# One hand-written list of steps replaced by another: attention and a Mish feed-forward on one core

## The chip, the cores and the metric

The kernel runs on one core of one Trainium2 chip. The metric is the device time of one execution in microseconds (us), the median of the runs. Lower is better.

## The reference, cut to what matters

Eight batches of eight heads go through attention in which a query sees few keys: in heads 0 to 3 the 32 latest positions, in heads 4 to 7 every fourth of the 128 latest. The result, 4608 tokens of 512 features, goes through a feed-forward layer with the Mish function.

```python
batch, n_heads, seq, head_dim = (8, 8, 576, 64)
mask_plain = (rel >= 0) & (rel < window)                                   # window = 32
mask_dil = (rel >= 0) & (rel < window * dilation) & (rel % dilation == 0)  # dilation = 4
scores = np.where(masks[None, :, :, :], scores, -1000000000.0)
attn = np.exp(scores - max) / (sum + 1e-09)
x = (attn @ v), tokens x 512
h = x @ w_in                        # 512 -> 2048
g = h * np.tanh(np.log1p(np.exp(np.minimum(h, 20.0))))
out = g @ w_out                     # 2048 -> 512
```

q, k and v come as 4-byte floats, w_in and w_out as 8-byte floats. The output has the precision of 4-byte floats, so large products are made of f16 halves: a high and a low part of each operand, three products for one.

## The kernel before, in words

**Units.** The work is cut into 16 units u, one for each half (288 positions) of each batch. A unit goes through these steps, each a Python function that issues a few instructions. Some are generators, and every further call of one issues its next piece:

- `ld`, `lv`: the loads of q, k and v. `pr` (`prep`, lines 440 to 540): scales, and the f16 halves of q, k, v; on ScalarE lines 508, 511, 517 and 536.
- `sp` (line 596 on TensorE), `sc` (scores to VectorE, maxima at line 626), `ex` (exponentials, ScalarE line 667 or 654), `tp` (transposes), `va` (line 744 or 738), `tx` (the attention result turned for the next product), one of each for a pair of heads. Units 0 to 3 are "direct": they use 4-byte products, since the f16 halves are not there so early.
- `ff` u.fp (`ff1`, line 840): two row blocks of `x @ w_in`, 12 products of 128x288 each, into both halves of one PSUM tile, then Mish on ScalarE (line 843). `gt` (`gate`, lines 859 and 861): the f16 halves of g.
- `fo` u.e.j (`ff2`, line 871): 12 products of `g @ w_out` for the output block e (0 to 3) and the quarter j of the inner dimension (0 to 3). Blocks 0 and 1 share one PSUM tile, blocks 2 and 3 another, each block one half (bank) of it. After j = 3 a second call moves the block to SBUF (`y`, ScalarE line 885, in four cases VectorE line 883), a third one stores it.
- `wl`, `wm`, `ww`, `ws`, `wp`: loads of the weights and their conversion from 8-byte floats to two f16 halves. On VectorE that is lines 380, 382, 383 and 395, on ScalarE lines 337 and 392.
- `kw` n (`keep_warm`, line 900): n products of zeros of 128x128 on TensorE, whose result nobody reads.

**PSUM.** All of these share four PSUM tiles, `banks`, named b0 to b3, each of two banks:

```python
banks = [ps.tile([P, 2, 512], F32, name=f"b{i}", bufs=1) for i in range(4)]
def take(name, tiles):
    turns[name] = place[0] if place else (turns.get(name, -1) + 1) % len(tiles)
    return tiles[turns[name]]
```

**Order.** No scheduler chooses: the list ORDER at the head of the file names the steps in the order in which they are issued, and each engine runs its instructions in that order. An entry such as `sp2.3=0` also says which of the four PSUM tiles the step takes. The waits between engines are put in by the framework from the tiles that an instruction reads and writes. The loop at the end walks the list:

```python
for name in ORDER:
    name, _, at = name.partition("=")
    place[:] = [int(at)] if at else []
```

In `ff2` both blocks of a pair write the same tile:

```python
if (e, j) == (e & 2, 0):
    d["po", e // 2] = take("b", banks)
po = d["po", e // 2][:, e % 2]
```

Of the kernel before, what the change touches and what calls it, by code (L numbers as in the profile page):

```python
# [42 lines left out]
va0.2 kw6=3 tx0.3 ex0.1 va0.2 sp1.1=3 tx0.3 sc1.1 sp1.2=2 sc1.2 tx0.2=0 tx0.2 tp0.1=1 wl0.2.0 wp0.0.1 kw10=3 sp1.0=3
sc1.0 tp0.1 va0.1=1 tx0.2 tx0.2 va0.1 va0.1 wl0.1.1 ex1.1 kw16=2 kw16=2 kw6=2 tp1.1=2 tp1.1 wm0.2.0 kw10=0 tx0.1=0
tx0.1 kw16=1 kw11=1 tx0.1 tx0.1 tx0.0=1 tx0.0 kw13=2 tx0.0 tx0.0 ww0.1.0 ww0.2.0 ww0.2.0 wm0.1.1 ex1.2 kw16=2 kw16=2
kw16=2 kw2=2 tp1.2=2 tp1.2 ww0.1.1 ww0.1.1 ex1.0 sp1.3=0 sc1.3 ex1.3 ws0.2=1 ws0.2 wp0.2.0 ww0.2.1 wp0.2.1 ws0.1=2
ws0.1 wp0.1.0 xa1 ld2 kw3=3 sp2.0=3 sc2.0 ex2.0 lv2 fs0 ff0.6=1 ff0.6 ff0.6 ff0.7=0 ff0.7 ff0.7 wp0.2.1 wl1.3.1
# [20 lines left out]
pr5 lv5 pr5 fo0.0.3 ff2.6=3 ff2.7=1 ff2.7 ff2.7 ff2.6 ff2.6 gt2.3=2 gt2.3 sc4.3 ex4.3 tp4.3=1 tp4.3 tp4.3=1 fs4
fo2.2.0=0 fo2.3.0 fo2.3.1 fo2.3.2 pr5=1 pr5 fo2.0.0=3 fo2.1.0 fs3 fo2.0.1 fo2.0.2 fo2.0.3 fo2.0.3 fo2.0.3 pr5 pr5 pr5
pr5 pr5 sp4.1=2 sc4.1 ex4.1 tp4.1=2 fo2.3.3 fo2.3.3 fo2.3.3 sp4.0=1 sc4.0 ex4.0 tp4.0=1 tp4.0 tp4.0=2 tx3.3=2 tx3.3  # L70
fo2.2.1 fo2.2.2 fo2.2.3 fo2.2.3 fo2.2.3 fo1.0.0=1 fo1.0.1 fo1.0.2 fo1.0.3 pr5 pr5 fo1.1.0 ld6 pr5 pr5 pr6 pr6 pr6
tx3.3 tx3.3 ff3.0=0 ff3.0 ff3.0 ff3.2=2 ff3.2 ff3.2 fo2.1.1 fo2.1.2 fo2.1.3 fo2.1.3 tp4.1 sp5.1=0 sp4.2=2 sc4.2 ex4.2
tp4.2=1 fo1.1.1 fo1.1.2 sc5.1 va4.3=3 sp5.3=2 sc5.3 va4.3 va4.3 ff3.1=0 ff3.1 ff3.1 gt3.0=3 gt3.0 ff3.3=2 ff3.3 ff3.3
gt3.1=1 fo2.1.3 fo1.0.3 fo1.1.3 lv6 pr6 pr6 pr6 tp4.1=0 va4.1=0 fo1.1.3 ex5.1 tp5.1=0 va4.1 va4.1 tx4.1=1 gt3.1 tx4.1
tx4.1 fo1.0.3 tp4.2 tp4.2=1 tx4.3=0 tx4.3 tx4.3 ff3.6=3 ff3.6 ff3.7=2 ff3.7 ff3.7 tp5.1 tp5.1=0 fo1.1.3 ff3.6 gt3.3=4
gt3.3 pr6 pr6 pr6 pr6 pr6 ff3.4=1 ff3.5=0 ff3.5 ff3.5 ff3.4 ff3.4 gt3.2=0 gt3.2 fo3.2.0=2 fo3.2.1 fo3.3.0 ld7 pr7 pr7
ex5.3 tp5.3=2 tp5.3 fo3.3.1 fs6 fo3.0.0=3 va4.0=0 tp5.3=2 va4.0 va4.0 tx4.0=1 tx4.0 tx4.0 fo3.1.0 fo3.1.1 sp6.1=1
# [5 lines left out]
tx5.0 va5.2=0 va5.2 tx5.3 tx5.3 ex6.2 tp6.2=2 tp6.2 tp6.2=2 va5.2 fo3.0.3 ff4.4=3 ff4.5=1 ff4.5 ff4.5 ff4.4 ff4.4
gt4.2=0 gt4.2 fo4.0.0=2 fo4.0.1 fo4.1.0 fo4.1.1 fo4.1.2 fo4.0.2 pr7 pr7 pr7 pr7 sp7.1=0 sc7.1 sp7.2=1 sc7.2 pr7
sp7.3=3 sc7.3 ex7.1 tp7.1=1 fo4.1.3 fo4.1.3 tx5.2=0 tx5.2 tx5.2 fo4.2.0=0 fo4.2.1 fo4.2.2 fo4.2.3 fo4.2.3 fo4.2.3
fo4.3.0 fo4.1.3 sp6.3=1 ex6.1 tp6.1=0 tp6.1 tp6.1=1 sc6.3 ex6.3 tp6.3=2 tp6.3 tp6.3=0 fo4.3.1 fo4.3.2 fo4.3.3 fo4.3.3
fo4.3.3 sp6.0=3 sc6.0 ex7.3 va6.2=1 va6.2 va6.2 tx6.2=1 ex6.0 ld8 fo4.0.3 fo4.0.3 tx6.2 tx6.2 fo4.0.3 pr8 tp6.0=0 pr8
# [871 lines left out]
```

## Time and profile before

| | |
|---|---|
| median of 3 runs | 964.04 us (962.53 to 965.33) |
| the profiled execution | 965.67 us, span of its instructions 963.7 us |
| mean granted TensorE clock | 0.987 |
| TensorE busy | 919.5 us, 95% of the span |
| VectorE busy | 592.6 us, 61% |
| ScalarE busy | 548.4 us, 57% |
| DMA queue of the program | 80.97 MB, 34.1% of 16 engines' span |

In the rows of the profile, PE is TensorE's matmul side, PEld its loading of weights, DVE is VectorE, ACT ScalarE, POOL GpSimd. A row of the timeline gives start, length, engine, line, operation, what is written and read, and in brackets how long the engine sat idle before it and what ended that. A row of the waits gives the engine and line that waited, what it waited for, the total, the number of times and the longest. In the table by stretches, PEclk is the clock that TensorE was granted, as a share of full speed. The chain of waits gives start, length and what took that time.

### The profile page before, as it was taken

To read this page: it belongs to the slowest core of one execution; us is meant where nothing else is said; L and a number is where in the kernel's file an instruction comes from. 1 tells how busy PE (TensorE), PEld (TensorE's weight loads), DVE (VectorE), ACT (ScalarE), POOL (GpSimd) and SP (SyncE) were. 2 spreads that over 40 slices of the span, in tenths; PEclk is the share of its full clock that TensorE was granted. 3 is DMA by queue.
4 is the path that set the end of the run, shared out by engine and by line. 5 is a ranking of instruction groups with operands and counts; after the bars stand their busy time and mean duration, and the time that the engine had idled before them with its cause. 6 is when DMAs were issued, how large, how long until landed. Compare 5 with 4: busy or idle time off the path is not lost.

```text
span 963.7 us, 21536 instructions
## 1 busy us (share of the span) xinstructions
PE 919.5 (95%) x9278; PEld 736.8 (76%) x9278; DVE 592.6 (61%) x879; ACT 548.4 (57%) x808; POOL 20.6 (2%) x99
## 2 busy tenths in 40 slices
PE   6899999998999999999998999999989999989998
PEld 4788888876878878788777878787867678768776
DVE  3896888575577675777785865665656366234120
ACT  3677675575383756676674655756364554744241
POOL 1000000210000000000000000000000000000000
PEclk9999999998999999999999999999989999999999
DMA  7756135032342324345344333172334121131200
GB/s 252 222 148 198 53 132 131 14 101 52 91 108 64 64 53 108 63 129 109 79 97 92 88 83 58 35 159 47 85 87 94 30 50 38 34 71 14 58 1 25
DMA packets 156558, 82.33 MB, mean 85 GB/s; under 512 B 122960, under 2 KB 152368, under 8 KB 156464
## 3 DMA queue, kind: packets, MB, share of 16 engines
q1 hardware_dynamic: 156464, 80.97, 34.1%
q8 instruction: 72, 1.18, 0.5%
q14 instruction: 22, 0.18, 0.1%
HBM read 49.02 MB, written 9.44 MB: 61 GB/s over the span
## 4 chain that ended last, share of the span: by engine, by line
PE 88%; ACT 5%; DVE 3%; issue 2%; DMA 1%; SPq 0%; POOL 0%; ACTq 0%; DVEq 0%; POOLq 0%
PE b L871 37%; PE b L840 37%; PE b L596 4%; PE b L744 3%; PE b L738 2%; PE b L900 2%; ACT y L885 1%; PE b L715 1%; PE b L593 1%; ACT g L859 1%; DMA knd<-in_kdT 1%; DVE nm L626 0%; ACT sb L667 0%; DVE sb L620 0%; PE b L348 0%
## 5 line engine op out<-in xcount | busy, mean ns | idle before, releaser
L871 PE MATMUL b<-g,w 128*128 128x288 f16 x3072 | 398.5, 290 | 27.7 <-ACT y L885 17.7
L840 PE MATMUL b<-x,w 128*128 128x288 f16 x3072 | 385.4, 286 | 0.0
L871 PEld LDWEIGHTS <-w 128*128 128x128 f16 x3072 | 300.6, 99 | 109.6 <-issue 30.0
L840 PEld LDWEIGHTS <-w 128*128 128x128 f16 x3072 | 298.4, 98 | 75.7
L861 DVE SCALAR_TENSOR_TENSOR g<-hm,sg,g 128x1152 f16<-128x1152 f32 x64 | 90.2, 1415 | 133.0 <-ACT g L859 132.8
L843 ACT ACTIVATE hm<-b,fs 128x576 f32<-128x576 f32 x128 | 92.6, 737 | 119.2 <-PE b L840 114.8
L885 ACT ACTIVATE y<-b,fo 128x288 f32<-128x288 f32 x60 | 42.1, 715 | 87.7 <-PE b L871 83.3
L859 ACT ACTIVATE g<-hm,sg 128x1152 f16<-128x1152 f32 x64 | 80.2, 1254 | 3.0 <-PE b L871 1.3
L667 ACT ACTIVATE sb<-sb,ln_p 72x576 f32<-72x576 f32 (+3 forms) x48 | 42.5, 890 | 42.6 <-DVE sb L628 42.4
L628 DVE TENSOR_TENSOR sb<-sb,nm 72x576 f32<-72x576 f32 (+4 forms) x60 | 45.3, 754 | 2.1
L626 DVE TENSOR_REDUCE nm<-sb 72x8 f32<-72x576 f32 (+4 forms) x60 | 44.9, 748 | 1.6
L620 DVE SCALAR_TENSOR_TENSOR sb<-b,sc,m_d 72x576 f32<-72x576 f32 (+1 forms) x24 | 22.6, 943 | 35.0 <-PE b L596 34.9
L759 DVE TENSOR_TENSOR xs<-b,rec 96x384 f32<-96x384 f32 (+1 forms) x64 | 39.7, 620 | 6.4 <-DVE rec L758 0.5
L620 DVE SCALAR_TENSOR_TENSOR sb<-b,sc,m_r 96x704 f32<-96x704 f32 (+1 forms) x24 | 23.4, 977 | 30.5 <-PE b L596 30.4
L705 DVE TENSOR_TENSOR p<-sb,p 72x576 f16<-72x576 f32 (+3 forms) x32 | 28.6, 898 | 15.9 <-ACT p L703 15.8
L843 ACT ACT_TABLE_LOAD x24 | 30.8, 1283 | 10.0 <-PE b L840 9.7
L596 PEld LDWEIGHTS <-q 64*72 64x72 f16 (+1 forms) x1008 | 25.9, 116 | 8.1 <-issue 7.8
L596 PE MATMUL b<-k,q 64*96 64x128 f16 (+3 forms) x1008 | 30.9, 210 | 0.0
L775 ACT CAST x<-xs 96x384 f16<-96x384 f32 (+1 forms) x27 | 15.1, 557 | 27.0 <-DVE xs L759 18.6
L754 ACT ACTIVATE den<-b 72x8 f32<-72x8 f32 (+1 forms) x48 | 7.9, 167 | 36.8 <-PE b L744 36.8
L758 DVE RECIPROCAL rec<-den 96x6 f32<-96x6 f32 (+1 forms) x64 | 12.0, 188 | 26.6 <-ACT den L754 22.4
L900 PE MATMUL b<-zeros 128*128 128x128 f16 x338 | 25.2, 235 | 3.2 <-ACT x L801 1.1
(140 smaller groups left out, 849.8 us busy)
## 6 DMA issues: line engine op xcount, KB each, us to landing
qn<-in_qT SPq DMA_DIRECT2D x16, 576.0 KB
out_T<-y SPq DMA_DIRECT2D x64, 144.0 KB
raw<-in_w_in SPq DMA_DIRECT2D x16, 512.0 KB
raw<-in_w_out SPq DMA_DIRECT2D x16, 512.0 KB
vn<-in_v SPq DMA_DIRECT2D x48, 128.0 KB
knd<-in_kdT SPq DMA_DIRECT2D x16, 208.0 KB
vdn<-in_vd SPq DMA_DIRECT2D x32, 104.0 KB
knp<-in_kT SPq DMA_DIRECT2D x8, 320.0 KB
```

The costliest lines, as they stand in the source:

```text
L596: nc.tensor.matmul(o, q, k, start=start, stop=stop, skip_group_check=True)
L620: nc.vector.scalar_tensor_tensor(args[0], args[1], d["sc"][:nq], args[2], ALU.mult, ALU.add)
L626: nc.vector.tensor_reduce(nm[:nq, :, j:j + n], x, axis=AX.X, op=ALU.max, negate=True)
L628: nc.vector.tensor_tensor(blocked(sb, c0, n, w), x, nm[:nq, :, j:j + n].unsqueeze(3).broadcast_to([nq, 2, n, w]), op=ALU.add)
L667: nc.scalar.activation(x, x, AF.Exp, bias=ln_p[:nq])
L840: nc.tensor.matmul(ph[:, h, :HT], w1[j][:, c, wi, k * P:(k + 1) * P], x_of(d, xi, c), start=(n == 0), stop=(n == len(seq) - 1))
L843: nc.scalar.activation(d["m"][j][:, k0:k0 + 2], ph[:, :, :HT], AF.Mish, scale=d["fs"][:, j:j + 1])
L859: nc.scalar.activation(g[:, 0], m, AF.Identity, scale=sg)
L861: nc.vector.scalar_tensor_tensor(g[:, 1], m, sg, g[:, 0], ALU.mult, ALU.subtract)
L871: nc.tensor.matmul(po[:, :HT], w2[:, e, j, wi, k * P:(k + 1) * P], d["g"][j][:, gi, k, :], start=(j == 0 and n == 0), stop=(j == NCH - 1 a ...
L885: nc.scalar.activation(o, src, AF.Identity, scale=fo)
L900: nc.tensor.matmul(warm[:, 1, 512 - P:], zeros, zeros, start=True, stop=True)
```

## The change

The list ORDER is replaced by another one. Nothing else differs: the functions, the tiles, the sizes and the engine of each step are the same. The old list has 2051 entries, the new one 2054. The three more are `kw` entries: 30 of them with 338 products of zeros before, 33 with 345 products now. Ahead of the first `sp` step there were 47 of these products, and there are 35. The new list was found by a search whose model takes a PSUM tile of two banks as one thing for waits.

```diff
 ORDER = """
-wl0.3.0 wm0.3.0 ww0.3.0 ww0.3.0 wl0.3.1 wm0.3.1 ww0.3.1 ld0 ww0.3.1 kw16=0 kw16=0 kw15=0 sp0.2=0 sc0.2 ws0.3=1 sp0.1=2
...
+ld0 kw16=0 kw16=0 kw3=0 sp0.1=0 sp0.2=1 sc0.1 sc0.2 sp0.0=2 sc0.0 sp0.3=3 sc0.3 wl0.3.0 wm0.3.0 ex0.2 ww0.3.0 ww0.3.0
```

How blocks of `fo` that share a tile stand to each other differs all through the list. In the old one the work on one block goes on, 25 times, behind the `y` of the other block of its tile, often with little between; around unit 7, for instance, `fo7.3.3 fo7.3.3 fo7.3.3 va8.1 tx8.1=0 tx8.1 tx8.1 pr11 pr11 pr11 fo7.2.1`. In the new one the even block of each of the 32 tiles is ended, with its `y`, before the odd one begins, with steps of other kinds or other tiles between, as in `fo7.2.3 fo7.2.3 fo7.2.3 sp10.0=2 sc10.0 va8.1=0 pr10 tp9.3=1 va8.1 pr10 lv11 va9.0=3 va9.0 va8.1 tx8.1=1 tx8.1 tx8.1 fo7.3.0`.

The first place is ScalarE while the output of unit 2 is made. Before, the queue stands as follows; `y` is the output block, the number behind `<-b` the PSUM tile, `qn`, `q2` and `k2` belong to the `pr` step of a later unit, `sb` and `p161` to its attention:

```order
L885 ACTIVATE y_2894<-b3_73,fo_1696 128x288
L508 ACTIVATE qn_2680<-qn_2680,s_2688 128x1152
L511 CAST q2_2905<-qn_2680 128x288 x2
L511 CAST q2_2905<-qn_2680 128x576
L517 ACTIVATE k2_2910<-knp_2682,s_2688 128x640
L517 ACTIVATE k2_2910<-knd_2684,s_2688 128x832
L667 ACTIVATE sb_2931<-sb_2931,ln_p_121 96x2x352
L703 CAST p161_2505<-sb_2931 96x2x352
L885 ACTIVATE y_2953<-b0_70,fo_1696 128x288
```

Now, on the same engine in the same unit:

```order
L885 ACTIVATE y_2923<-b3_73,fo_1623 128x288
L885 ACTIVATE y_2956<-b0_70,fo_1623 128x288
L508 ACTIVATE qn_2599<-qn_2599,s_2629 128x1152
L511 CAST q2_3018<-qn_2599 128x288 x2
L511 CAST q2_3018<-qn_2599 128x576
L517 ACTIVATE k2_3023<-knp_2601,s_2629 128x640
L517 ACTIVATE k2_3023<-knd_2603,s_2629 128x832
L536 ACTIVATE vh_3031<-vn_2616,s_2629 128x12x64
L536 ACTIVATE vdh_3032<-vdn_2617,s_2629 104x16x64
L843 ACTIVATE hm_2884<-b2_72,fs_2865 128x576
```

The `y` of tile b0 stood behind the whole `pr` step; it now stands ahead of it.

The second place is the head of VectorE's queue. `nm` are the maxima of unit 0's scores, `w13` and `raw` belong to the first weights. Before:

```order
L293 MEMSET ones_111 128x1
L891 MEMSET ln_p_121 128x1
L895 MEMSET zeros_123 128x64
L380 TENSOR_SCALAR w13_105<-w13_105 128x1024
L382 SCALAR_TENSOR_TENSOR raw_127<-raw_127,w13_105 128x1024
L383 SCALAR_TENSOR_TENSOR raw_127<-raw_127 128x1024
```

Now:

```order
L895 MEMSET zeros_123 128x64
L626 TENSOR_REDUCE nm_187<-b0_70 96x2x2
L626 TENSOR_REDUCE nm_187<-b0_70 96x2
L626 TENSOR_REDUCE nm_190<-b1_71 72x8
L626 TENSOR_REDUCE nm_200<-b2_72 96x2x2
L626 TENSOR_REDUCE nm_200<-b2_72 96x2
L626 TENSOR_REDUCE nm_213<-b3_73 72x8
L380 TENSOR_SCALAR w13_105<-w13_105 128x1024
L382 SCALAR_TENSOR_TENSOR raw_215<-raw_215,w13_105 128x1024
L383 SCALAR_TENSOR_TENSOR raw_215<-raw_215 128x1024
```

The conversion of the first weights moved behind all the maxima of unit 0.

More of the change, by code (lines that the diff above doesn't have):

```diff
@@ L43 @@
[L43 to L47, printed above, removed]
@@ L68 @@
[L68 to L72, printed above, removed]
@@ L73 @@
[L73 to L77, printed above, removed]
@@ L83 @@
[L83 to L87, printed above, removed]
@@ new lines @@
+fo2.3.0 fo2.3.1 fo2.3.2 fo2.3.3 fo2.3.3 ex4.1 fo2.1.3 pr6 pr6 pr6 pr6 pr6 pr6 fo2.3.3 sp4.2=2 sc4.2 xa6 ex4.3 tp4.3=1
+tp4.3 tp4.3=1 sp5.2=1 fo1.0.0=3 fo1.0.1 fo1.0.2 fo1.0.3 fo1.0.3 fo1.0.3 sp4.0=0 sc4.0 ex4.0 tp4.0=2 tp4.0 tp4.0=2
+sc5.2 ff3.1=2 ff3.1 ff3.1 gt3.0=1 gt3.0 fo1.1.0 fo1.1.1 fo1.1.2 fo1.1.3 fo1.1.3 fo1.1.3 pr6 pr6 pr6 pr6 pr6 ld7 pr7
+ff3.4=0 ff3.5=2 ff3.5 ff3.5 ff3.4 ff3.4 gt3.2=3 gt3.2 ff3.6=1 ff3.6 ff3.6 ff3.7=3 ff3.7 ff3.7 gt3.3=2 gt3.3 va4.0=2
+va4.0 va4.0 ff3.3=0 ff3.3 ff3.3 gt3.1=0 gt3.1 fo3.2.0=1 fo3.0.0=3 tx4.0=1 tx4.0 tx4.0 tp4.1=1 tp4.1 tp4.1=0 ex4.2
@@ new lines @@
+gt4.1 sp6.2=1 sc6.2 va5.0=0 va5.0 va5.0 tp5.2=0 ff4.1 ff4.1 gt4.0=1 gt4.0 va5.3=2 va5.3 va5.3 tp6.1=2 ff4.6=1 ff4.6
+ff4.7=3 ff4.6 xa5 tx5.0=1 tx5.0 tx5.3=0 tx5.3 tx5.3 tx5.0 va5.2=0 va5.2 va5.2 va5.1=1 va5.1 va5.1 ff4.7 ff4.7 gt4.3=0
+gt4.3 pr7 tp6.1 tp6.1=2 sp6.0=2 sc6.0 ex6.2 tp6.2=0 tp6.2 tp6.2=0 ff4.4=0 ff4.5=1 ff4.5 ff4.4 ff4.5 ff4.4 gt4.2=3
+gt4.2 fo4.2.0=3 fo4.2.1 fo4.0.0=2 fo4.0.1 fo4.0.2 fo4.0.3 fo4.2.2 pr7 pr7 pr7 pr7 sp7.3=1 pr7 ld8 sc7.3 tx5.2=0 tx5.2
+tx5.2 fo4.2.3 sp6.3=0 sc6.3 tx5.1=1 tx5.1 sp7.1=1 sc7.1 fo4.0.3 pr8 fo4.0.3 fo4.1.0 fo4.2.3 fo4.2.3 fo4.3.0 ex6.3
@@ new lines @@
+tx12.3=1 tx12.3 tx12.3 pr13 pr13 lv14 ff11.5 ff11.5 ff11.4 pr14 gt10.3 ff11.6=1 ff11.6 ff11.6 ff11.7=3 ff11.7 ff11.7
+fo10.2.0=2 fo10.2.1 fo10.2.2 fo10.2.3 tx12.2 ex13.3 tp13.3=2 tp12.0=0 va12.0=0 va12.0 fo10.2.3 fo10.2.3 sp13.1=1
+sc13.1 fo10.0.0=3 fo10.0.1 fo10.0.2 fo10.0.3 va12.0 tp13.3 pr14 pr14 fo10.0.3 fo10.0.3 ex13.0 tp13.0=0 tp13.0 tp13.0=2
+ex13.1 tp13.1=1 fo10.3.0 va12.1=1 va12.1 tx12.0=1 tx12.0 tx12.0 fs13 fo10.1.0 gt11.3=4 fo10.1.1 fo10.1.2 fo10.1.3
+fo10.1.3 gt11.3 fo10.3.1 gt11.1=2 gt11.1 fo10.3.2 fo10.3.3 fo10.3.3 gt11.2=0 gt11.2 fo11.0.0=0 fo11.2.0=3 fo11.0.1
@@ new lines @@
+fo11.0.2 fo11.0.3 ex13.2 tp13.2=0 fo11.2.1 fo11.2.2 fo11.2.3 va12.1 tx12.1=1 tx12.1 pr14 pr14 fo10.3.3 fo11.0.3
+fo11.0.3 tx12.2 xa13 tp13.1 tp13.1=0 fo11.1.0 fo11.1.1 pr14 tx12.1 pr14 pr14 sp14.0=2 pr14 pr14 va13.0=1 fo11.2.3
+fo11.2.3 fo11.3.0 sc14.0 va13.1=2 va13.1 va13.1 tp13.3=1 tx13.1=0 fo10.1.3 va13.0 ex14.0 va13.0 fo11.3.1 fo11.3.2
+fo11.3.3 fo11.3.3 sp14.2=2 sc14.2 ex14.2 fo11.1.2 tp13.2 sp14.1=1 sc14.1 ex14.1 tp14.1=1 ld15 lv15 pr15 pr15 pr15 pr15
+pr15 pr15 tp13.2=2 ff12.0=3 ff12.0 ff12.0 tp14.1 ff12.1=2 ff12.1 ff12.1 tp14.2=2 tp14.2 tp14.2=0 tp14.0=0 tp14.0
@@ new lines @@
+fo11.3.3 gt12.0=1 xa14 ff12.2=1 ff12.2 ff12.2 ff12.3=3 ff12.3 ff12.3 gt12.1=3 gt12.1 tx13.0=1 tx13.0 va13.3=2 va13.3
+va13.3 tx13.0 pr15 pr15 fo11.1.3 fo11.1.3 ff12.4=1 ff12.5=3 ff12.5 ff12.5 ff12.4 ff12.4 gt12.2=2 gt12.0 tx13.1
+va14.2=2 va14.2 va14.2 tx13.1 fo11.1.3 tx13.3=1 tx13.3 tx13.3 va13.2=0 va13.2 va13.2 tx13.2=0 tx13.2 gt12.2 ff12.6=3
+ff12.7=1 ff12.7 ff12.7 ff12.6 ff12.6 gt12.3=0 gt12.3 fo12.0.0=2 fo12.0.1 fo12.0.2 fo12.0.3 fo12.2.0=0 fo12.0.3
+fo12.1.0 fo12.1.1 fo12.1.2 tp14.1=1 pr15 pr15 pr15 pr15 tx14.2=1 tp14.0=0 tx13.2 tx14.2 sp14.3=1 sc14.3 fo12.1.3
@@ new lines @@
+sp15.2=1 sc15.2 ex15.2 tp15.2=0 tp15.2 tp15.2=0 ff13.6=0 ff13.7=3 ff13.7 ff13.7 ff13.6 ff13.6 gt13.3=2 gt13.3 fs14
+ff14.0=2 ff14.0 ff14.0 ff14.2=1 ff14.1=3 ff14.2 ff14.2 ff14.1 tp15.0=2 gt13.1 ff14.6=0 ff14.6 tp15.3=2 va15.3=2 va15.3
+va15.3 ex15.1 tp15.1=0 tp15.1 tp15.1=1 fo13.2.0=1 fo13.2.1 fo13.2.2 ff14.6 ff14.1 ff14.3=2 tp15.0 gt14.0=0 gt14.0
+tp15.0=2 ff14.4=0 ff14.3 ff14.3 tx15.3=1 tx15.3 ff14.4 ff14.4 fo13.2.3 fo13.2.3 fo13.2.3 ff14.5=3 ff14.5 va15.1=2
+va15.1 va15.1 tx15.1=0 tx15.1 tx15.1 tx15.3 fo13.0.0=0 fo13.0.1 fo13.0.2 va15.2=2 va15.2 ff14.5 fo13.0.3 fo13.0.3
@@ L165 @@
+ff15.6 fo13.3.3 fo13.3.3 fo13.3.3 ff15.1=3 ff15.1 ff15.1 gt15.0=4 gt15.0 ff15.3=2 ff15.3 ff15.3 gt15.1=3 gt15.1
+ff15.7=0 ff15.7 ff15.7 gt15.3=1 gt15.3 fo15.2.0=1 fo15.0.0=3 fo15.0.1 fo15.2.1 fo15.2.2 fo15.2.3 fo15.2.3 fo15.0.2
+fo15.0.3 fo15.0.3 fo15.3.0 fo15.3.1 fo15.3.2 fo15.2.3 fo15.3.3 fo15.3.3 fo15.0.3 fo15.3.3 fo15.1.0 fo15.1.1 fo15.1.2
+fo15.1.3 fo15.1.3 fo15.1.3
 """.split()
```

198 lines of the change are left out of this document (92 added, 106 removed).

## The prediction

> **What bounds the kernel now.** I read the page first, then TensorE's waits, then its timeline at single waits, then the chain and the clock.
>
> ```profile
> span 963.7 us, 21536 instructions
> PE 919.5 (95%) x9278; PEld 736.8 (76%) x9278; DVE 592.6 (61%) x879; ACT 548.4 (57%) x808; POOL 20.6 (2%) x99
> ...
> L871 PE MATMUL b<-g,w 128*128 128x288 f16 x3072 | 398.5, 290 | 27.7 <-ACT y L885 17.7
> L840 PE MATMUL b<-x,w 128*128 128x288 f16 x3072 | 385.4, 286 | 0.0
> ```
>
> TensorE (PE) is busy for 919.5 of 963.7 us, so the order of steps can only win what lies outside those 919.5 us, which is 44.2 us, and whatever of the busy time is slow or useless. The two feed-forward products make up 784 us of it. They are alike in shape, yet one never waits and the other waits 27.7 us. So the question is what line 871 waits for. The waits of PE alone, from 100 us to the end:
>
> ```profile
> PE b L871 <- ACT y L885: 17.7, 11, 4.6
> PE b L871 <- ACT den L754: 6.2, 2, 3.9
> PE b L871 <- ACT fs L824: 2.5, 1, 2.5
> PE b L871 <- DVE y L883: 1.3, 1, 1.3
> ```
>
> This is the whole answer for that stretch: after 100 us PE waits 15 times, 27.7 us in all, only at line 871, and 12 of the 15 times by name for `y`, the move of a finished output block out of PSUM. (The other three, `den` and `fs`, are small ScalarE instructions that stand behind a `y` in its queue: in the old list the waiting products are `fo10.0.1`, `fo11.0.1` and `fo13.0.2`, which follow the `y` of block 1 of their tile. I count them as the same wait.) The last wait of the program shows which block it is:
>
> ```profile
> 955.75 1.63 PE L871 MATMUL b<-g,w 128*128 128x288 f16 x12
> ...
> 957.47 0.77 ACT L885 ACTIVATE y<-b,fo 128x288 f32<-128x288 f32 x1 [9.03 <-PE b L871]
> ...
> 958.28 1.63 PE L871 MATMUL b<-g,w 128*128 128x288 f16 x12 [0.90 <-ACT y L885]
> ```
>
> In the old list the last products are `fo15.3.3`, and the `y` just before them is that of `fo15.2.3`. Block 2 and block 3 have different banks, and nothing of block 3 is read by the `y` of block 2. Still PE stands idle until it ends. So the program's waits go by the tile of two banks. That is a wait with no other sense, and it costs 0.90 us where ScalarE is free at once. Where ScalarE has a queue, it costs more. Here is the longest one, from the timeline of both engines:
>
> ```profile
> 224.42 1.25 ACT L508 ACTIVATE qn<-qn,s 128x1152 f32<-128x1152 f32 x1 [0.63 <-DVE s L286]
> ...
> 226.27 0.47 PE L786 MATMUL b<-ident,xs 72*128 72x72 f32 x4
> ...
> 228.25 0.97 ACT L517 ACTIVATE k<-knd,s 128x832 f16<-128x832 f32 x1
> ...
> 230.76 0.49 ACT L885 ACTIVATE y<-b,fo 128x288 f32<-128x288 f32 x1
> ...
> 231.30 4.88 PE L871 MATMUL b<-g,w 128*128 128x288 f16 x21 [4.56 <-ACT y L885]
> ```
>
> The `y` of b0 stands behind `qn`, `q2` and `k2` of a later unit, which is the queue shown in the first place of the change. PE loses 4.56 us. And it loses more after that, since its clock falls:
>
> ```profile
> 220.00:240.00 20.00, 15.44 (x135) 11.39 (x134) 11.79 (x24) 11.41 (x16) 0.00 (x0) 0.83 0.22 50
> 500.00:520.00 20.00, 16.32 (x148) 12.49 (x146) 13.31 (x24) 13.02 (x20) 0.78 (x6) 0.91 0.62 121
> 700.00:720.00 20.00, 16.06 (x130) 11.99 (x128) 13.50 (x16) 14.24 (x20) 0.29 (x4) 0.83 0.21 55
> 740.00:760.00 20.00, 17.77 (x173) 13.76 (x168) 5.00 (x8) 6.94 (x10) 0.00 (x0) 0.91 0.07 23
> 840.00:860.00 20.00, 16.27 (x151) 12.23 (x149) 8.75 (x11) 8.52 (x14) 0.00 (x0) 0.92 0.42 86
> ```
>
> The third number from the end of a row is PEclk. It falls below full speed in these five stretches, each of which holds one of the long waits at line 871. The chain shows what the same work takes there:
>
> ```profile
> 133.00 4.41 PE b L871 x36
> 231.30 14.06 PE b L871 x96
> 508.54 6.24 PE b L871 x36
> 708.50 7.04 PE b L871 x36
> 751.22 6.18 PE b L871 x36
> 858.97 24.26 PE b L840 x192
> 911.81 23.52 PE b L840 x192
> ```
>
> **The change part by part.**
>
> *The waits for `y` (a gain of 27.7 us, less what is left).* In the new list each of the 32 even blocks is ended and its `y` issued before the odd block of that tile begins. So 32 places can wait. What hides each is the PE work between the last product of the even block and the first of the odd one. The least of it is at `fo8.0.3` (a `va` and an `sp` step, 18 to 24 products each) and at units 12 and 14 (one `fo`, 12 products).
>
> ```profile
> 255.91 1.05 PE b L596 x42
> 320.52 1.29 PE b L744 x42
> ```
>
> At 1.05/42 and 1.29/42 us a product, 24 of each make 0.6 + 0.7 = 1.3 us. Twelve feed-forward products are 4.41/3 = 1.47 us. Both are more than the 0.90 us that a free ScalarE takes. In the old list 8 such places have no other PE work between at all. If ScalarE is late by its queue, cover of this size doesn't do: at 231.30 PE had 18 products of line 596 and 4 of line 786 to do, and still waited 4.56 us. But in the new list `pr` and its like stand behind the `y`, as the first place shows. Nine of the 32 places have less than 2.2 us of cover by my count of the list. I allow **1.5 us** for them together, a sixth of a microsecond each. The bounds are 0 (all hidden) and 32 x 0.90 = 29 us (no cover works).
>
> *The clock (a gain of 10.4 us).* At full speed 36 products take 4.41 us, so 96 take 11.76 us. The excess is 14.06 - 11.76 = 2.30, 6.24 - 4.41 = 1.83, 7.04 - 4.41 = 2.63 and 6.18 - 4.41 = 1.77 us, together 8.53. The fifth is the wait before 856.41:
>
> ```profile
> 856.41 2.56 PE L871 MATMUL b<-g,w 128*128 128x288 f16 x12 [2.54 <-ACT fs L824]
> ...
> 624.94 1.63 PE L871 MATMUL b<-g,w 128*128 128x288 f16 x12 [1.81 <-ACT y L885]
> ```
>
> Twelve products took 2.56 us there, against 1.63 in the same form of row elsewhere, which is 0.93 more, and the 192 behind them 24.26 - 23.52 = 0.74 more. The sum is 10.2; I take **10.2 us**. The wait of 1.81 us at 624.94 left the clock whole, the one of 2.54 us did not. If no wait of over 2 us is left in the new order, all 10.2 us come back. If two are, some 4 of them stay lost.
>
> The Trainium skill ("TensorE: Matmul & The Clock Gate", Part 1: The HAM clock gate) says that the clock falls to half after an idle window of about 3.4 us. By that rule alone the wait of 2.54 us and the shorter one of `den`, 6.2 - 3.9 = 2.3 us, would have cost no speed, and this term would be 2.30 + 1.83 + 2.63 = 6.8 us, 3.4 us less than I take. The rows of this trace decide: the stretch at 856 us is slow after 2.54 us of idle time.
>
> *The products of zeros (a loss of 1.1 us).*
>
> ```profile
> 55.78 2.79 PE b L900 x50
> 14.15 0.64 PE L593 MATMUL b<-m_fb,ident_b 72*72 72x288 bf16 x2 [7.91 <-ACT m_fb L250]
> ```
>
> One takes 2.79/50 = 0.056 us. Ahead of the first scores there were 47 and are 35. These lie in time that PE loses anyway, since the first scores wait until 14.15 us for the mask `m_fb`, which comes from GpSimd and ScalarE and is not moved. Behind that point there were 291 and are 310, so 19 x 0.056 = **1.1 us**. If they lie where PE would have waited, they cost nothing (0 to 1.1).
>
> *The first weights (a loss of 1 us).*
>
> ```profile
> 8.82 0.69 DVE L380 TENSOR_SCALAR w<-w 128x1024 int32<-128x1024 int32 x1 [7.83 <-ACT w L337]
> ...
> 17.07 0.75 DVE L626 TENSOR_REDUCE nm<-b 72x8 f32<-72x576 f32 x1
> ...
> 20.00:40.00 20.00, 17.45 (x179) 13.87 (x178) 14.75 (x29) 11.05 (x17) 0.00 (x0) 1.00 0.70 234
> 40.00:60.00 20.00, 20.00 (x304) 18.07 (x303) 18.19 (x23) 12.50 (x23) 0.27 (x3) 1.00 0.79 222
> ```
>
> In the old order VectorE (DVE) converted the first weights from 8.82 us on, while PE waited for the mask. In the new one (the second place) its queue begins with the maxima of all four score tiles, which can't come before 14.15 us. So VectorE starts some 6 us later. What stands behind it are the splits of the first weights, and the first feed-forward products wait for those. From 20 to 60 us VectorE is busy for 14.75 + 18.19 of 40 us, so it has 7 us in which it can make up for 6 us; also, in the old order its maxima waited for scores that now come early. I take **1 us**, with bounds of -4 (the scores being early helps more) and +6 (none of it is made up for). The loads of the first unit go ahead of those of the first weights in SP's queue, which moves the same bytes in another order and is part of this term.
>
> *The rest.* All other steps are the same instructions elsewhere. What hides them is PE's own 919.5 us: VectorE and ScalarE have 371 and 415 us free. The old order shows no wait of PE after 100 us for Mish, gates, scores or values, and I take none for the new one. If that cover goes, it is a rival below.
>
> Sum, on the span: 963.7 - 27.7 - 10.2 + 1.5 + 1.1 + 1.0 = 929.4 us. The profiled execution took 965.67 us, 1.97 more than its span and 1.63 above the median of the runs, 964.04. Against the median the sum is 964.04 - 34.3 = 929.7, rounded to **929.5 us**.
>
> **The rivals.**
>
> *The waits come back elsewhere.* The new order packs ScalarE and VectorE work into stretches that are 34 us shorter, and PE may now wait for Mish (line 843), a gate or a `va`. Against it speaks that the L840 row has 0.0 us of idle time, though ScalarE's queue was as long as at 224 us. For it speaks that every wait of over 2 us brings about 2 us of slow clock with it. With four such waits of 2 us, each with 10.2/5 = 2 us of lost speed behind it, half of the gain goes: 929.5 + 16 = 945.5 us (937.5 with two, 953.5 with six).
>
> *The change doesn't do what it says.* If a wait were not by the tile but by the bank, the moves of `y` would touch nothing, and PE's waits at line 871 would be for `g`. The time would be 964.04 + 1.1 + 1 = 966 us, within 0.3% of before. The row at 958.28 speaks against it: the gates of unit 15 were all done before the first `fo15`, and PE waited for `y` by name. The Trainium skill ("PSUM — Partial Sum Buffer", PSUM bank collisions raise a hardware error) asks for guards by bank and quadrant only, so the chip itself would not need this wait; the trace shows that the program has it.
>
> *Slower: PSUM tiles run short.* In the new order block pairs 0/1 and 2/3 of a unit are often open at once, for instance around `fo4.0.3` and `fo4.2.3`, and hold two of the four tiles until both odd blocks end. All `ff`, `sp`, `va` of that time must go through the other two, and each of them then waits for the engine that empties the tile before it, at 0.9 us as for `y`. There are 128 `ff` steps. It decides from 34.5/0.9 = 38 such waits on; with 60 of the 128 it would be 929.5 + 54 = 983.5 us. Against it: the old order had the same pairs open (`fo2.0` and `fo2.2`), with no wait at line 840 in 3072 products.
>
> **How the numbers follow.** I give the forecast 86%, waits elsewhere 9%, no effect 2%, slower 3%. Within the forecast the time goes from 929.5 - 1.5 - 1.1 - 5 = 922 to 929.5 + 5 (first weights) + 6 (four times the 1.5 us that I put on the covered places, with no slow clock) = 940.5. The range takes in the lower part of the first rival as well: 922 to 943 us. What a measurement of this kernel can tell from no change is about 0.3%, 2.9 us. Faster by more than that are the forecast and waits elsewhere, 0.95; the same 0.02; slower 0.03.
>
> **What would show it.** Right: in the waits of PE after 100 us, line 871 for `y` has under 3 us instead of 27.7; PEclk is 1.00 in all stretches from 100 us on; the busy time of PE is about 910 us, since the slow stretches are gone; the first line 840 starts near 63 us, as it does now:
>
> ```profile
> 63.38 0.79 PE L840 MATMUL b<-x,w 128*128 128x288 f16 x5
> ```
>
> Wrong: line 840 or 744 shows idle time, with Mish or VectorE as its releaser (waits elsewhere); line 871 still has over 20 us (no effect); the first line 840 starts after 70 us (first weights); or any stretch after 100 us has a PEclk under 1.

## The result, and the profile after

The changed kernel takes **931.62 us** (median of 4 runs, 927.91 to 935.97), the one before, measured beside it, 963.4 us (4 runs, 962.53 to 965.33). The ratio is 0.9669, with a 95% interval of 0.9621 to 0.9718. The profiled run took 933.42 us, and its span is 931.6 us, 32.1 less than before. The page has TensorE's totals and the two feed-forward products:

```profile
span 931.6 us, 21552 instructions
PE 911.0 (98%) x9285; PEld 735.0 (79%) x9285; DVE 592.3 (64%) x879; ACT 541.0 (58%) x800; POOL 22.6 (2%) x99
...
L871 PE MATMUL b<-g,w 128*128 128x288 f16 x3072 | 388.3, 286 | 0.0
L840 PE MATMUL b<-x,w 128*128 128x288 f16 x3072 | 387.8, 286 | 0.0
```

Line 871 now has the mean of line 840, 286 ns (it had 290), and its 27.7 us of idle time are 0.0. All that PE waits for from the first line 840 (68.63 us) to the end is this, in the waits of that stretch:

```profile
PE b L900 <- ACT sb L661: 0.9, 1, 0.9
PE b L786 <- DVE xs L759: 0.4, 1, 0.4
PE b L900 <- DVE m L470: 0.2, 1, 0.2
PE b L900 <- DVE xs L759: 0.2, 1, 0.2
PE b L799 <- ACT x L796: 0.2, 1, 0.2
```

No `y` is among them. How the new list does that can be read at the timeline of PE and ScalarE, at one of the moves of a block:

```profile
230.33 1.63 PE L871 MATMUL b<-g,w 128*128 128x288 f16 x12
...
231.91 3.10 PE L871 MATMUL b<-g,w 128*128 128x288 f16 x24
232.00 0.50 ACT L885 ACTIVATE y<-b,fo 128x288 f32<-128x288 f32 x1 [0.68 <-PE b L871]
...
237.46 1.91 ACT L511 CAST q<-qn 128x288 f16<-128x288 f32 x3
```

The `y` runs from 232.00 on, and PE is at products of another tile from 231.91 on. The casts of `pr` stand behind the `y`. In the table by stretches, the five that had a lowered clock, and the first two of the span:

```profile
0.00:20.00 20.00, 10.86 (x87) 8.39 (x89) 2.66 (x8) 4.38 (x6) 2.85 (x17) 0.71 0.83 253
20.00:40.00 20.00, 18.23 (x166) 14.17 (x165) 15.50 (x24) 8.82 (x13) 0.00 (x0) 0.78 0.34 119
...
220.00:240.00 20.00, 20.00 (x197) 15.83 (x195) 13.25 (x25) 5.77 (x11) 0.00 (x0) 1.00 0.03 9
500.00:520.00 20.00, 20.00 (x242) 16.31 (x242) 16.35 (x29) 14.16 (x22) 1.23 (x5) 1.00 0.36 89
700.00:720.00 20.00, 20.00 (x191) 15.99 (x190) 12.28 (x15) 12.90 (x16) 0.00 (x0) 1.00 0.38 66
740.00:760.00 20.00, 20.00 (x219) 16.39 (x216) 12.16 (x18) 12.94 (x19) 0.30 (x3) 1.00 0.47 93
840.00:860.00 20.00, 20.00 (x194) 16.18 (x191) 4.89 (x8) 7.22 (x11) 0.00 (x0) 1.00 0.17 39
```

PEclk is 1.00 in the later five, and PE is busy there for all 20 us. It is 0.71 and 0.78 in the first 40 us. PE's timeline of the start shows products at half speed too (12 products of line 596 take 1.49 us there, and 0.85 us at full speed in a run below):

```profile
13.05 0.74 PE L593 MATMUL b<-m_fb,ident_b 96*96 96x352 bf16 x2 [8.09 <-ACT m_fb L250]
13.73 1.49 PE L596 MATMUL b<-knp,qn 64*96 64x128 f32 x12
...
20.91 4.54 PE L648 MATMUL b<-nm,ident 72*72 72x288 f32 x12
...
68.63 1.63 PE L840 MATMUL b<-x,w 128*128 128x288 f16 x12
```

A slow start is not new with this list. Before, the table gives a PEclk of 1.00 for the first 40 us, but the same 12 products took as long:

```profile
18.29 1.49 PE L596 MATMUL b<-knp,qn 64*96 64x128 f32 x12
```

So in the first stretches the durations say more than PEclk. The prediction has no term for this half clock in either list. It ends at about 24 us before and at about 29 us now.

The first line 840 starts at 68.63 us instead of 63.38. So the start lost 5.2 us, and what comes behind it went from 963.7 - 63.4 = 900.3 to 931.6 - 68.6 = 863.0 us, a gain of 37.3 us. The net is 32.1.

### The profile page after: what moved, and what is told of

It reads as the page before. It is cut to its first block, busy times and chain, and to the rows that moved or that the text cites. A ratio compares the mean times of both kernels' runs of the same rounds, so it can differ in the third digit from the quotient of the medians.

```text
span 931.6 us, 21552 instructions
## 1 busy us (share of the span) xinstructions
PE 911.0 (98%) x9285; PEld 735.0 (79%) x9285; DVE 592.3 (64%) x879; ACT 541.0 (58%) x800; POOL 22.6 (2%) x99
## 4 chain that ended last, share of the span: by engine, by line
PE 96%; issue 1%; ACT 1%; DVE 1%; POOL 0%; DVEq 0%; ACTq 0%; POOLq 0%
PE b L871 41%; PE b L840 40%; PE b L596 4%; PE b L744 3%; PE b L900 2%; PE b L738 2%; PE b L648 1%; PE b L715 1%; PE b L593 1%; PE b L351 0%; PE b L348 0%; PE b L786 0%; PE b L799 0%; ACT x L801 0%; PE b L308 0%
## 5 line engine op out<-in xcount | busy, mean ns | idle before, releaser
L871 PE MATMUL b<-g,w 128*128 128x288 f16 x3072 | 388.3, 286 | 0.0
L667 ACT ACTIVATE sb<-sb,ln_p 96x704 f32<-96x704 f32 (+3 forms) x48 | 42.2, 886 | 33.9 <-DVE sb L628 33.8
L705 DVE TENSOR_TENSOR p<-sb,p 96x704 f16<-96x704 f32 (+3 forms) x31 | 27.7, 897 | 15.6 <-ACT p L703 15.4
L520 DVE TENSOR_TENSOR q<-qn,q 128x288 f16<-128x288 f32 (+1 forms) x36 | 23.4, 701 | 13.3 <-ACT q L511 13.3
L900 PEld LDWEIGHTS <-zeros 128*128 128x128 f16 x345 | 23.6, 107 | 10.5 <-issue 8.0
L620 DVE SCALAR_TENSOR_TENSOR sb<-b,sc,m_r 96x704 f32<-96x704 f32 (+1 forms) x24 | 23.4, 976 | 12.0 <-PE b L596 11.9
L596 PE MATMUL b<-k,q 64*96 64x128 f16 (+3 forms) x1008 | 30.7, 210 | 0.0
L626 DVE TENSOR_REDUCE nm<-b 96x4 f32<-96x512 f32 (+4 forms) x20 | 14.7, 749 | 20.3 <-PE b L596 20.3
```

What stands on the lines that cost most here:

```text
L596: nc.tensor.matmul(o, q, k, start=start, stop=stop, skip_group_check=True)
L620: nc.vector.scalar_tensor_tensor(args[0], args[1], d["sc"][:nq], args[2], ALU.mult, ALU.add)
L626: nc.vector.tensor_reduce(nm[:nq, :, j:j + n], x, axis=AX.X, op=ALU.max, negate=True)
L667: nc.scalar.activation(x, x, AF.Exp, bias=ln_p[:nq])
L871: nc.tensor.matmul(po[:, :HT], w2[:, e, j, wi, k * P:(k + 1) * P], d["g"][j][:, gi, k, :], start=(j == 0 and n == 0), stop=(j == NCH - 1 a ...
L900: nc.tensor.matmul(warm[:, 1, 512 - P:], zeros, zeros, start=True, stop=True)
```

## The experiments

The first run is the changed kernel itself. The other nine kernels differ from one of the two lists by their list alone, so each computes the whole result. Their lists are written on fewer lines, so a line of a function has a number two lower than in the kernels above (four lower in the one without zeros): line 871 is 869 there, 885 is 883, 840 is 838.

### The new list once more

No edit: it is the changed kernel.

> The new list once more, unchanged. Its four runs so far spread from 927.91 to 935.97 us with a granted clock of 1.0, 0.999, 0.988 and 0.987, while those of the old list stay within 962.53 to 965.33. If the spread comes from how long TensorE's clock stays at half at the start of the program, the runs with a clock near 1.0 are the short ones again (about 928 against 934 us), and the first row of line 840 moves with it between profiles. If it comes from something later, time and clock don't go together.

Measured: 932.86 us (929.52 to 937.51), ratio 0.9698 (0.9644 to 0.9752). Its span is 928.0 us, 3.6 less than that of the first profile. The start in its timeline:

```profile
20.53 2.40 PE L648 MATMUL b<-nm,ident 72*72 72x288 f32 x12
```

The same 12 products of line 648 that took 4.54 us take 2.40 here. The products reach full speed at about 20 us instead of 29 us, and the first line 840 starts at 64.96 us. From there to the end it is 928.0 - 65.0 = 863.0 us, the same as in the first profile. So these two profiles differ by how long the start runs at half clock, and not behind it. For the other runs that is not shown. The sign that had been named for it, short times with a mean granted clock near 1.0, did not come: 937.51 us went with a clock of 1.000, and 929.52 us with 0.994. But the mean clock misses part of the start: it is 1.000 in this profile too, though its products ran at half speed until 20 us.

### The cover of the `y` taken away, in the new list

At 26 of the 32 places the first piece of the odd block is put right behind the `y` of the even one. At 17 of them no other TensorE work is then left between the two blocks; at the rest some stands ahead of the `y`. All steps and products stay.

```diff
-fo2.0.3 fo2.0.3 fo2.0.3 pr5 pr5 pr5 pr5=1 fo2.2.2 fo2.2.3 fo2.2.3 pr5 pr5 pr5 fo2.1.0
+fo2.0.3 fo2.0.3 fo2.1.0 fo2.0.3 pr5 pr5 pr5 pr5=1 fo2.2.2 fo2.2.3 fo2.2.3 fo2.3.0 pr5 pr5 pr5
 ...
```

> The new list, with the first product block of each odd output block (fo u.odd.0, units 2 to 15) put right behind the y of the even block of its tile, so that at 17 places no other TensorE work stands between. Waits by the two-bank tile: each of the 17 places waits 0.9 us or more, 15 us in all at line 871, time about 931.6 + 15 = 947 us (943 to 955, more where ScalarE has a queue or a long wait brings the slow clock). Waits by the bank: no wait at line 871, time within 3 us of the new list.

Measured: 962.9 us (959.21 to 966.31, 10 runs), ratio 0.9993 (0.9968 to 1.0018). The whole gain is gone; the time is 16 us above the 947 us that had been worked out. The waits of PE, and the longest of them in the timeline of PE and ScalarE:

```profile
PE b L869 <- ACT y L883: 24.0, 21, 4.8
```

```profile
414.55 0.77 ACT L883 ACTIVATE y<-b,fo 128x288 f32<-128x288 f32 x1 [0.16 <-PE b L869]
...
417.12 0.78 ACT L665 ACTIVATE sb<-sb,ln_p 72x576 f32<-72x576 f32 x1 [1.06 <-DVE sb L626]
417.93 0.67 ACT L701 CAST p<-sb 72x576 f16<-72x576 f32 x1
418.51 0.76 ACT L883 ACTIVATE y<-b,fo 128x288 f32<-128x288 f32 x1
...
419.32 3.01 PE L869 MATMUL b<-g,w 128*128 128x288 f16 x12 [4.80 <-ACT y L883]
```

This is the picture of the old list again: the `y` stands behind exponentials in ScalarE's queue, PE waits 4.80 us for it, and then 12 products take 3.01 us instead of 1.63, since the clock has fallen. Eleven of the 21 waits are the plain ones of 0.85 to 0.86 us, and five are of 1.6 us or more. In the table by stretches:

```profile
400.00:420.00 20.00, 14.34 (x148) 11.06 (x146) 11.41 (x16) 13.24 (x18) 0.00 (x0) 0.98 0.53 133
420.00:440.00 20.00, 20.00 (x187) 15.35 (x186) 15.00 (x24) 8.50 (x12) 0.38 (x1) 0.93 0.05 16
700.00:720.00 20.00, 16.98 (x151) 12.94 (x149) 8.33 (x14) 6.26 (x9) 1.40 (x1) 0.91 0.11 23
```

The part behind the first line 838 (70.78 us) is 964.5 - 70.8 = 893.7 us, 30.7 more than with the cover. Of these, 24.0 are the waits and (0.02 + 0.07 + 0.09) x 20 = 3.6 the clock. About 3 are left. Over 21 waits that is 0.14 us each, close to the 0.16 us by which a row of 12 products (1.63 us) exceeds 12 products within a longer row (4.41/3 = 1.47 us). So each break seems to cost the run-out of the last product once; no run tests that by itself. The rule by tiles is shown: with the bank as the measure there would have been no wait. The price of a wait is its length, about 0.14 us more, and some 1.8 us where the clock falls behind it (3.6 us for two). So the estimate of 947 us was short by the waits with a queue ahead of the `y`, by the places with part of their cover left, and by the clock. The profiled run is the longest of the ten; its span holds another 5.8 us of a slower start than in the second run of the new list (70.78 against 64.96).

### The `y` covered in the old list

The old list, with its own start. At 13 of the 15 places where PE waited, steps of other tiles that came later are drawn ahead of the waiting products.

```diff
-fo7.2.1 fo7.2.2 fo7.2.3 fo7.2.3 fo7.2.3 va9.0=3 va9.0 va9.0 tp9.3=1 tp10.1=0 pr11 fo7.0.0=2 fo7.0.1 pr11 fs11 fo7.1.0
+va9.0=3 fo7.0.0=2 fo7.0.1 fo7.1.0 fo7.2.1 fo7.2.2 fo7.2.3 fo7.2.3 fo7.2.3 va9.0 va9.0 tp9.3=1 tp10.1=0 pr11 pr11 fs11
 ...
```

> The old list, in which at 13 of the 15 places where line 871 waited some TensorE work of other tiles (1.2 to 5.9 us of it) is drawn ahead of the waiting products; start and all the rest as before. Two places of 0.85 and 0.90 us are left. If the waits for y and the slow clock behind them were the whole gain: 963.4 - 26 - 10 = 927.5 us, as fast as the new list or faster. If the new list's gain came from its start or from the new order as a whole: near 960 us. If drawing work ahead only moves the waits: 940 to 955 us with idle time at lines 840 or 744.

Measured: 932.45 us (931.15 to 934.46), ratio 0.968 (0.9647 to 0.9714). These few moves give the gain of the whole new list in the median, though 5 us less than the 927.5 us that had been worked out. What is left at line 869:

```profile
PE b L869 <- ACT y L883: 1.8, 2, 0.9
PE b L869 <- DVE sb L618: 1.7, 1, 1.7
PE b L869 <- DVE xs L757: 1.3, 1, 1.3
PE b L869 <- ACT fs L822: 0.9, 1, 0.9
```

The two `y` waits of 0.9 us are the two places that were not covered. The one for `fs` is probably what is left of the wait of 2.54 us. The two for VectorE are new: some of the waits only moved, to a PSUM tile that VectorE had not emptied, and the one of 1.7 us brought the slow clock with it (PEclk 0.91 from 220 to 240 us). The first product of line 838 starts at 60.70 us, so the part behind it is 930.2 - 60.7 = 869.5 us, 6.5 more than in the new list, and the start is 4.3 to 7.9 us shorter. So the new list is better behind the start, and its longer start takes this away again.

### More zeros in the wait for the mask, in the new list

120 more products of zeros behind the 35 at the head. They lie in the 8 us in which PE waits for `m_fb`.

```diff
-ld0 kw16=0 kw16=0 kw3=0 sp0.1=0
+ld0 kw16=0 kw16=0 kw3=0 kw16=0 kw16=0 kw16=0 kw16=0 kw16=0 kw16=0 kw16=0 kw8=0 sp0.1=0
```

> The new list with 120 more products of zeros ahead of the first scores, where TensorE waits 8.1 us for the mask in any case. If the start is long because the clock is at half from 8 to 28 us: the clock stays full through the wait, the first scores run at full speed, the first row of line 840 comes 4 to 7 us earlier than 68.6 us, time about 926 us, and less spread. If the start is bound by the conversion of the first weights on VectorE: the first row of line 840 stays at 67 to 69 us and the time within 3 us.

Measured: **926.65 us** (925.62 to 928.3), ratio 0.962 (0.9587 to 0.9652). All four runs lie below the four of the new list measured beside them (929.52 to 937.51), though not all below the lowest of its first four (927.91). The start in PE's timeline:

```profile
1.05 11.10 PE L898 MATMUL b<-zeros 128*128 128x128 f16 x155 [1.05 <-DVE zeros L893]
12.96 0.46 PE L591 MATMUL b<-m_fb,ident_b 96*96 96x352 bf16 x2 [0.81 <-ACT m_fb L248]
13.35 0.85 PE L594 MATMUL b<-knp,qn 64*96 64x128 f32 x12
...
17.41 2.40 PE L646 MATMUL b<-nm,ident 72*72 72x288 f32 x12
```

The wait is 0.81 us instead of 8.09. The first scores take 0.85 us instead of 1.49, and the products of the maxima 2.40 instead of 4.54. The first line 838 starts at 63.45 us. The best and the worst run are 2.7 us apart, where the new list has 8.0. So the half clock of the start was worth 5 to 6 us of the median. This kernel has the lowest median of all, but the interval of its ratio still overlaps slightly with that of the new list (0.9644 to 0.9752).

### No zeros at all, in the new list

All 345 products of zeros (33 entries) are left out. Nobody reads their result, so what is computed stays whole.

```diff
-ld0 kw16=0 kw16=0 kw3=0 sp0.1=0
+ld0 sp0.1=0
 ...
```

> The new list without any of the 345 products of zeros. If they only lengthen TensorE's queue: 345 x 0.056 us = 19 us at the most, of which those behind the first scores, 310 x 0.056 = 17 us, could be won: 915 to 925 us. If they only fill time in which TensorE waits for the weights' conversion: within 4 us of 932. If they are what holds the clock up: slow stretches all through the first 100 us, the first row of line 840 no earlier than 68 us, 932 to 942 us.

Measured: 936.95 us (935.56 to 937.87), ratio 0.9719 (0.9704 to 0.9733). The waits of PE, and its timeline:

```profile
PE b L589 <- ACT m_fb L246: 13.8, 1, 13.8
```

```profile
30.80 4.47 PE L644 MATMUL b<-nm,ident 96*96 96x256 f32 x12
...
48.50 1.60 PE L592 MATMUL b<-knp,qn 64*96 64x128 f32 x12
...
73.01 2.24 PE L836 MATMUL b<-x,w 128*128 128x288 f16 x17
```

The second set of line 644 runs at half clock too (4.47 us; 2.35 in the kernel with more zeros), and so do the products up to about 60 us: those at 48.50 us take 1.60 us, where the same form took 0.90 at full speed before (43.33 us). The first line 836 starts at 73.01 us. So the third case came: the zeros hold the clock up in the first 60 us. The median is 4 to 5 us higher than the new list's, but three of that list's eight runs (935.96, 935.97 and 937.51 us) lie in the same range, so a loss in time is not shown.

### The first weights ahead of the scores

The kernel with 120 more zeros, and both halves of the first weights loaded and converted before the first scores. This was to test whether the start is longer because VectorE begins with the maxima.

```diff
-ld0 ... sp0.1=0 sp0.2=1 sc0.1 sc0.2 sp0.0=2 sc0.0 sp0.3=3 sc0.3 wl0.3.0 wm0.3.0 ex0.2 ww0.3.0 ww0.3.0 wl0.3.1 wm0.3.1 ww0.3.1 ww0.3.1
+ld0 wl0.3.0 wm0.3.0 ww0.3.0 ww0.3.0 wl0.3.1 wm0.3.1 ww0.3.1 ww0.3.1 ... sp0.1=0 sp0.2=1 sc0.1 sc0.2 sp0.0=2 sc0.0 sp0.3=3 sc0.3 ex0.2
```

> The new list with 120 more products of zeros ahead of the first scores (926.65 us, first row of line 840 at 63.45 us) and, besides, the loads and the conversion of the first weights (both halves of 0.3) put directly behind the loads of unit 0, ahead of unit 0's maxima on VectorE, as the old list has them. If the start is bound by VectorE, which is nearly always busy from 14 to 56 us there: it gets 6 us of its work done while TensorE waits for the mask, TensorE's waits for ScalarE and VectorE in the first 65 us (6 us) shrink, 921 to 924 us. If TensorE's own queue with its zeros sets the start: within 1.5 us of 926.65.

Measured: 935.98 us (934.78 to 939.85), ratio 0.9717 (0.9693 to 0.9741): slower than the kernel it was made from. The waits of PE and VectorE's timeline:

```profile
PE b L646 <- DVE nm L624: 4.7, 1, 4.7
```

```profile
13.12 0.69 DVE L378 TENSOR_SCALAR w<-w 128x1024 int32<-128x1024 int32 x1 [12.13 <-ACT w L335]
...
19.38 3.14 DVE L624 TENSOR_REDUCE nm<-b 96x4 f32<-96x512 f32 x6
```

The conversion on ScalarE (line 335) still stood behind the mask, so VectorE began at 13.12 us and not at 8.8 as in the old list. PE waited 4.7 us for the maxima and lost its clock once more: the 12 products behind that wait took 4.51 us instead of 2.40. The 921 to 924 us that an early VectorE would have given did not come. With 44 zeros behind that place left out, it was no different:

> As the one before, without the 44 products of zeros that stand between unit 0's exponentials and the sum over the first weights (2.5 us at full clock). If VectorE bounds the start: VectorE's next maxima come 2.5 us earlier and it has no work waiting there, so the time is 1 to 3 us less than with them. If later waits take it all up: within 1 us. If the clock falls for it: 2 to 4 us more.

Measured: 935.31 us (933.78 to 936.1), ratio 0.9701 (0.9686 to 0.9715).

### Half of the first weights at the very head

The kernel with 120 more zeros, but `wl0.3.0 wm0.3.0 ww0.3.0 ww0.3.0` stand ahead of `ld0`, and so ahead of the mask on ScalarE.

```diff
+wl0.3.0 wm0.3.0 ww0.3.0 ww0.3.0
 ld0 ... sp0.3=3 sc0.3
-wl0.3.0 wm0.3.0
 ex0.2
-ww0.3.0 ww0.3.0
```

> The new list with 120 more products of zeros ahead of the first scores (926.65 us), and the load and conversion of the first half of the first weights (0.3.0) at the very head of the list, ahead of the loads of unit 0. There it stands ahead of the mask on ScalarE too, as in the old list, so that VectorE does 3.15 us of work between 8 and 14 us, where it is idle now. If VectorE bounds the start: the first row of line 840 comes at 60 to 61 us instead of 63.45, about 924 us. If the maxima of unit 0 are set back by it as in the kernel with both halves first: a wait of TensorE for nm and a time over 928 us. If TensorE's own queue sets the start: 926 to 927.5 us.

> As the one before, without the 44 products of zeros ahead of the sum over the first weights. If VectorE has caught up there and waits for that sum: 1 to 3 us less than with them. If the zeros only fill a wait: within 1 us. If the clock falls: 2 to 5 us more.

Measured: 929.44 us (927.9 to 936.13), ratio 0.9664 (0.9622 to 0.9707); without the 44 zeros 932.71 us (926.85 to 933.84), ratio 0.9668 (0.9637 to 0.97). VectorE's timeline of the first of them, and PE's:

```profile
8.84 0.69 DVE L378 TENSOR_SCALAR w<-w 128x1024 int32<-128x1024 int32 x1 [7.85 <-ACT w L335]
```

```profile
14.38 0.46 PE L591 MATMUL b<-m_fb,ident_b 96*96 96x352 bf16 x2 [1.76 <-DMA vdn<-in_vd]
...
64.77 11.92 PE L838 MATMUL b<-x,w 128*128 128x288 f16 x96
```

Here VectorE does begin at 8.84 us, as in the old list. But the scores start at 14.38 us instead of 12.96, and the first line 838 at 64.77 instead of 63.45. The maxima are thus set back as well, so this does not test an early start of VectorE alone. VectorE then waits 2.89 us for line 346 on PE, which stands behind the 44 zeros. Without these zeros that wait is 0.43 us, and line 838 starts at 61.72 us, 1.7 us earlier than in the kernel with 120 more zeros. But that profile is of the shortest of its four runs (926.85 us). The other three took 932.59 to 933.84 us, at a mean clock of 0.990 to 0.991 instead of 0.998, and the median is no better.

### The covered old list with more zeros ahead

The kernel with the old list covered, and 112 more zeros ahead of its first scores.

```diff
 ... ww0.3.1
+kw16=0 kw16=0 kw16=0 kw16=0 kw16=0 kw16=0 kw16=0
 kw16=0 kw16=0 kw15=0 sp0.2=0
```

> The old list with the 13 places covered (932.45 us) and 112 more products of zeros ahead of the first scores. There the clock came up at 17 us in the profile and the first row of line 840 at 60.7 us. If the half clock at the start is worth as much there as in the new list: the first scores run at full speed from 14 us, 1 to 3 us less, 929.5 to 931.5 us. If that start waits for VectorE: within 1 us of 932.45.

Measured: 931.5 us (930.53 to 932.42), ratio 0.9663 (0.9647 to 0.968), the same as without them within their spread. Its first line 838 starts at 60.26 us, against 60.70. In the profile without them, the old start came to full clock at about 18 us by itself, so there was little to win. Between the two lists with more zeros ahead, the start differs by 63.45 - 60.26 = 3.2 us.

## Why the prediction was right, step by step

It said 929.5 us, 922 to 943, and 931.62 was measured. That the sum came so close is in part luck, since errors cancel. On the span, 34.3 us were forecast and 32.1 gained: the waits brought 0.7 us more than forecast, the clock and the breaks 1.7 more, the zeros 0.4 less and the start 4.2 less. By its steps:

*The waits for `y`* (27.7 us gained, 1.5 left over). Right, and shown from both sides: taking the cover away brings 24.0 us of waits back and 962.9 us, and covering the old list's places gives 932.45 us. Nothing was left over at line 871, where 1.5 us had been allowed for. Other waits behind the first line 840 grew instead, from 1.1 us before to the 1.9 us of the rows above:

```profile
PE b L900 <- ACT x L801: 1.1, 1, 1.1
```

*The clock* (10.2 us). The mechanism is right: PEclk is 1.00 in all five stretches. (The heading of that part says 10.4 us; the sum uses 10.2.) Together with the 0.16 us that a break seems to cost, which the prediction had not counted, what it brought is 37.3 - 27.7 + 0.8 + 1.5 (the next term) = 11.9 us. The ten short waits of before times 0.16 us make 1.6, so 10.3 us are left for the clock. This split is worked out, not measured by itself.

*The products of zeros* (1.1 us lost). The groups by line from the first line 840 to the end, after and before:

```profile
L900 PE MATMUL b<-zeros 128*128 128x128 f16 x71 | 5.2, 219 | 1.4 <-ACT sb L661 0.9 <-DVE m L470 0.2 <-DVE xs L759 0.2
```

```profile
L900 PE MATMUL b<-zeros 128*128 128x128 f16 x50 | 3.7, 219 | 1.1 <-ACT x L801 1.1
```

21 more of them lie in that part, for 5.2 - 3.7 = 1.5 us at most. As a whole the zeros are no loss: with all of them left out the median is 4 to 5 us higher, within the spread of the new list. The prediction priced the added ones and did not ask what they hold up, which is the clock of the first 60 us.

*The first weights* (1.0 us lost, -4 to +6). This term of the sum was mis-sized: the start lost 5.2 us in the profiled run and 1.6 in the second one, within the bounds, and the sign that was named, a first line 840 near 63 us, did not come. Two causes act on the start, and the prediction had one of them. The other is the half clock of the start. It lasts to about 20 or to 29 us with the same list and is worth 68.63 - 64.96 = 3.7 us between these two. It is there in the old list as well, to about 24 us. Zeros in the wait for the mask let the first scores run at full speed; a fall of some 3 us at 57 us is left (PEclk 0.93 from 40 to 60 us). What remains, 3.2 us between the two lists with more zeros ahead, may be the order of the first weights, as the prediction had it: VectorE comes to their conversion (line 380) at 21.70 us instead of 8.82. But the trials that put the weights first did not win it back in the median. One was slower by 9 us (6.5 in the profiles), with a wait of 4.7 us for the maxima; the other started VectorE as early as the old list, but set the scores back by 1.4 us. Its profile without the 44 zeros is 1.7 us better at the first line 838, the median of that kernel is not. So VectorE's late start is neither shown nor excluded as the cause, and what makes up these 3.2 us stays open.

*The rivals.* Waits elsewhere: 1.9 us in 863 us, so no. No effect: no. PSUM tiles running short: line 840 has 0.0 us of idle time in 3072 products, so no. That the `y` of one bank holds back products into the other bank, on which the forecast rested, is confirmed in both lists.

## What to carry to other kernels

Where two users share a tile, the framework's wait goes by the tile: end one user and do work of other tiles before the other begins, and look at what stands ahead of the releasing instruction in its own engine's queue, since that sets the length of the wait. A long wait costs more than its length where the clock falls behind it, so long waits are to be filled first. And idle TensorE time at the start that can't be avoided can be filled with products that nobody reads: here that was worth 5 to 6 us in one list, and nothing clear in the covered old one.

## What the runs showed of the hardware that was not expected

**The clock falls after short waits, and their length alone does not decide.** Among the feed-forward products it fell after waits of 2.16 us (taken-away cover, at 709 us), 2.23 us (before, at 751 us) and longer, and not after 1.68 us (taken-away cover) or 1.81 us (before). In the covered old list it fell after 1.72 us:

```profile
225.78 6.49 PE L869 MATMUL b<-g,w 128*128 128x288 f16 x38 [1.72 <-DVE sb L618]
```

A row of 38 such products takes 4.82 us at full clock (line 838 at 241.05 us in the same run). Among the small products of the start it fell after still less. The first row is from the new list, the second from the one with the cover taken away:

```profile
63.38 1.05 PE L900 MATMUL b<-zeros 128*128 128x128 f16 x16 [1.46 <-ACT pp L724]
63.95 1.49 PE L898 MATMUL b<-zeros 128*128 128x128 f16 x16 [1.46 <-ACT pp L722]
```

The same wait of 1.46 us ahead of the same products left the clock whole in one run and not in the other, where PEclk is 0.91 from 60 to 80 us. The shortest wait with a fall behind it is 1.29 us (half of the first weights at the head, without the 44 zeros: the same 16 products take 1.87 us). So from 1.3 to 1.8 us both happen. The Trainium skill ("TensorE: Matmul & The Clock Gate", Part 1: The HAM clock gate) puts an idle window of about 3.4 us ahead of the fall, and says that the window runs freely. These runs show falls after single waits of 1.29 to 1.72 us, about half of that and less.

**The clock can stay low while TensorE works.** From 13.05 to 25.45 us the first profile of the new list has PE busy without a wait, on small products most of which have 4-byte operands, and the products at the end of that stretch still ran at half speed (4.54 us against 2.40). The same page of the Trainium skill names about 3.4 us of sustained work for the return to full speed; here 12 us did not do it in one profile, and some 6 us did in the other. What decides it is not shown. Where zeros fill the 8-us wait, the first scores run at full speed, and the four runs lie within 2.7 us.
